# Sinkhorn attention and token mixer on one core: 21 idle TensorE products in place of 8 in the opening

## The chip, the cores and the metric

The kernel runs on one core of a Trainium2 chip. The metric is the device time of one execution in microseconds (us); of several runs the median counts. Inputs and output lie in the chip's DRAM as float32, and the kernel computes in bf16 with float32 accumulation.

## The reference, cut to what matters

```python
# q, k, v: (4, 8, 768, 64); sort_net: (4, 8, 8, 8); w_q, w_k: (512, 64); w_out: (512, 512)
P = sort_net
for _ in range(5):
    P = exp(P - max(P, -1)); P = P / sum(P, -1); P = P / sum(P, -2)
k_sorted = einsum('bhij,bhjcd->bhicd', P, k_blocks)      # 8 blocks of 96 rows
v_sorted = einsum('bhij,bhjcd->bhicd', P, v_blocks)
scores   = q_blocks @ k_sorted_blocks.T / 8
x        = softmax(scores) @ v_sorted_blocks             # heads side by side: (4, 768, 512)
wq, wk   = x @ w_q, x @ w_k
mixed    = (wq @ wk.T / 8) @ x
out      = relu(mixed) @ w_out
```

## The kernel before, in words

The work goes batch by batch (b = 0 to 3). For each batch the blocks of K and V of its eight heads are mixed by the sort matrix P, which is written as a 128-by-128 matrix M for each head, so that the mixing is one TensorE product per head and row group. The order of all work is written out by hand in the table `ORDER` (line 18). An entry names a step, the batch, a number, and, behind colons, an engine (A, D, G, S for ACT, DVE, POOL, SP) or a PSUM bank. A capital letter is a step of TensorE, a small letter mostly the step that follows it on another engine. Each engine runs its own entries strictly in the order of the table and waits for another engine only where data or a buffer is shared.

The prediction speaks only of the opening, batch 0, up to some 20 us. Its steps are:

- `c00` to `c05` (DVE) and `a01` to `a05` (ACT, the exponential): five rounds of normalising the 32 matrices of sort_net, one behind the other. The last, `c05`, ends with a transpose into `PbT` (line 208).
- `A00` (line 190): eight small products, which need `idb`, the identity that POOL makes.
- `Z0n:bank` (line 269): n products of `fil`, a zeroed piece of the tile `mixT`, 128x128 weights and 512 columns, into a PSUM bank. No step reads what they write. The number behind `Z0` is their count.
- `z10` to `z13` (POOL, and ACT for `z13`): casts of Q, head pair by head pair, into `Qn`; `Q00` to `Q03` (line 275): six transposes each on TensorE; `q00` to `q03`: their copies to `QT`.
- `U00`, `U01` (line 347): transposes of the weights w_q and w_k; `z01`, `z02` their copies on ACT.
- `B00` (line 247): eight small products of `PbT` and `Lx`, which spread P over 128 partitions, in bank 6; `n03, n00, n02, n01` (DVE, line 257): the four parts of `M`, from that bank.
- `Y03, Y00, Y02, Y01` (line 308): the sort matrix's products with V, 12 each, with casts `y03` and `y02` on ACT and `y00` and `y01` on DVE into a K-shaped tile `KT`; `u00` (ACT) keeps bank 6 as `PTR` for the later batches.
- `F00, F03` (line 314): eight transposes of that tile each, copied by `f00` (ACT) and `f03` (DVE) into `VT`.
- `K03, K00, K02, K01` (line 302): the sort matrix's products with K, 12 each, with casts `k03, k02` (ACT) and `k00, k01` (DVE). Then the scores `S`, the exponentials `e`, and so on through the batch.

All products are issued from one helper, `mm` (line 164), so all TensorE rows have L165; the copies have L169 (ACT), L171 (POOL) and L173 (DVE). K, V and Q of each batch, and the weights, are loaded by POOL's DMA queue (`u_l`, line 233), one load behind the other; SP's queue brings sort_net and Q of batch 0, sends the sorted V of the later batches from `Vs` into `VT`, and writes the output.

```python
    def u_Z(b, n, bank):
        w, x = (idb, wqk.rearrange("p t d -> p (t d)")) if b else (fil[:, 0:P], fil)
        for _ in range(n):
            mm(PS[:, bank, :], w, x)
```

Of the kernel before, what the change touches and what calls it, by code (L numbers as in the profile page):

```python
# [15 lines left out]
SPQ = 2  # L16

ORDER = """
i02:D i00:G c00:D a01:A i03:G A00:3 Z04:2 Z02:0 c01:D lp a02:A:3 c02:D a03:A lv0 lk0 c03:D z10:G
a04:A Q00:5 q00:A:5 Z02:6 c04:D U00:0 z13:A z11:G lv1 Q01:4 a05:A z01:A:0 q01:A:4 c05:D Q03:1 U01:3  # L20
z12:G q03:D:1 Q02:2 B00:6 z02:A:3 n03:D:6 n00:D:6 Y03:0 n02:D:6 Y00:4 q02:A:2 y03:A:0 n01:D:6
u00:A:6 y00:D:4 Y02:2 Y01:0 F00:4 y02:A:2 F03:5 K03:6 K00:2 y01:D:0 f03:D:5 K02:0 f00:A:4 k03:A:6
k02:A:0 k00:D:2 K01:4 S05:6 S06:2 e05:A:6 e06:A:2 k01:D:4 F02:0 S04:4 F01:1 lk1 S03:6 e04:A:4 P04:2
lq1 S02:4 e03:A:6 n11:D f02:D:0 lk2 lv2 e02:A:4 n10:G f01:D:1 r04:D:2 V12:0 V11:6 x04:D:2 v11:A:6
# [702 lines left out]
```

## Time and profile before

| | |
|---|---|
| time, median of 3 runs | 98.2 us (97.89 to 98.4) |
| the profiled execution's own time | 98.7 us |
| its span in the profile | 96.5 us |
| TensorE products (PE) | busy 86.2 us, 89% of the span |
| ACT | busy 72.9 us, 76% |
| DVE | busy 70.9 us, 73% |
| read from DRAM, written | 20.19 MB, 6.29 MB |

The span is the time from the first to the last instruction that the profiler saw; the rest of the execution's time lies around it. Times in the rows are counted from the start of the span. A row of the timeline gives start, length, engine, line, operation, what is written and read, shape and count; the bracket at its end is idle time of the engine just before, and what ended it. A matmul's recorded length includes the time for its result to come out, so a group of n products is n times their spacing, and a tail.

### The profile page before, as it was taken

The numbers are of one execution on the slowest core, as the hardware profiler recorded it, in microseconds if no ns is written. First come the engines' busy times: TensorE is split into PE (matmuls) and PEld (weight loads), VectorE is DVE, ScalarE is ACT, GpSimd is POOL, SyncE is SP. The second block draws the span as 40 slices with busy tenths as digits, with TensorE's granted clock in tenths as the row PEclk, the third lists the DMA queues.
The fourth block names the chain that finished last, engine by engine and source line by source line (L and its number), as shares of the span: only waits on it lengthen the run. The fifth ranks groups of instructions, "written<-read, shape, count | busy, mean of one in ns | idle before, by whom it ended". The sixth has DMA issues, their size and how long they took to land.

```text
span 96.5 us, 3360 instructions
## 1 busy us (share of the span) xinstructions
PE 86.2 (89%) x1416; PEld 61.0 (63%) x1416; DVE 70.9 (73%) x137; ACT 72.9 (76%) x106; POOL 25.8 (27%) x48
## 2 busy tenths in 40 slices
PE   4709979999999988999999999999999999999950
PEld 2105879787889677885855877786576465554430
DVE  2677777899998699898942799968899782657010
ACT  5236956999897997895999978998981787648640
POOL 7986997100018991000000000000200182000000
PEclk9999999999999999999999999999999999999999
DMA  0899999999999999999999999684783369383983
GB/s 7 272 385 201 203 204 203 206 203 208 202 221 249 250 208 205 206 208 211 238 253 225 203 205 123 150 283 132 200 312 143 91 196 404 127 329 138 385 323 140
DMA packets 22351, 20.88 MB, mean 216 GB/s; under 512 B 5056, under 2 KB 20416, under 8 KB 22336
## 3 DMA queue, kind: packets, MB, share of 16 engines
q0 software_dynamic: 12256, 9.31, 62.3%
q1 hardware_dynamic: 9792, 10.83, 34.8%
q10 hardware_dynamic: 288, 0.52, 1.5%
q8 instruction: 11, 0.18, 0.7%
q14 instruction: 4, 0.03, 0.1%
HBM read 20.19 MB, written 6.29 MB: 274 GB/s over the span
## 4 chain that ended last, share of the span: by engine, by line
PE 69%; DVE 19%; ACT 3%; issue 3%; DMA 2%; ACTq 0%; DVEq 0%
PE ps L165 69%; DVE X L409 4%; DMA ot<-in_sort_net_dram 2%; DVE Pm L201 1%; DVE tmp L204 1%; ACT Pm L183 1%; DVE Vs L173 1%; DVE qkT L173 1%; DVE tmp L199 1%; DVE tmp L200 1%; DVE tmp L205 1%; ACT E L380 1%; DVE KT L173 1%; ACT ot L169 1%; DVE QT L173 1%
## 5 line engine op out<-in xcount | busy, mean ns | idle before, releaser
L380 ACT ACTIVATE E<-ps 96x960 bf16<-96x960 f32 (+1 forms) x28 | 23.8, 903 | 1.7 <-PE ps L165 1.5
L165 PE MATMUL ps<-wo,mixT 128*128 128x512 bf16 (+1 forms) x100 | 23.3, 371 | 0.0
L409 DVE TENSOR_TENSOR X<-ps,Rall 96x896 bf16<-96x896 f32 (+1 forms) x20 | 19.8, 1002 | 0.5
L165 PEld LDWEIGHTS <-mixT 128*128 128x128 bf16 x108 | 9.8, 101 | 10.0 <-issue 1.5
L169 ACT COPY ot<-ps 128x512 f32<-128x512 f32 (+2 forms) x18 | 10.3, 575 | 5.1 <-PE ps L165 4.9
L169 ACT CAST KT<-ps 128x768 bf16<-128x768 f32 x13 | 10.1, 804 | 2.3 <-PE ps L165 2.2
L165 PE MATMUL ps<-idb,Qn 128*64 128x128 bf16 (+1 forms) x168 | 8.5, 234 | 3.1 <-POOL Qn L171 3.1
L173 DVE COPY ot<-ps 128x512 f32<-128x512 f32 (+1 forms) x8 | 5.3, 657 | 7.8 <-PE ps L165 6.5
L165 PEld LDWEIGHTS <-KT 64*128 64x128 bf16 (+1 forms) x288 | 8.7, 98 | 3.3 <-issue 1.9
L165 PE MATMUL ps<-VT,E 96*128 96x65 bf16 x256 | 10.6, 193 | 0.2 <-DMA VT<-Vs 0.2
L165 PEld LDWEIGHTS <-E 96*128 96x128 bf16 x256 | 9.2, 97 | 2.4 <-issue 0.7
L165 PE MATMUL ps<-QT,KT 64*128 64x96 bf16 x256 | 9.3, 204 | 0.6 <-DVE wk L173 0.3
L165 PEld LDWEIGHTS <-Qn 128*64 128x64 bf16 (+1 forms) x168 | 6.9, 114 | 4.6 <-POOL Qn L171 4.0
L472 ACT ACTIVATE mixT<-ps 128x1024 bf16<-128x1024 f32 x7 | 7.2, 1030 | 2.6 <-PE ps L165 2.6
L171 POOL COPY qD<-qkT 64x384 bf16<-64x384 bf16 x1 | 0.5, 499 | 31.6 <-ACT qkT L169 31.6
L265 POOL TENSOR_TENSOR M<-PTR,m_p 128x512 bf16<-128x512 bf16 x4 | 5.2, 1310 | 12.4 <-PE ps L165 11.8
L173 DVE CAST KT<-ps 128x768 bf16<-128x768 f32 x7 | 6.5, 954 | 1.2 <-PE ps L165 1.2
L165 PE MATMUL ps<-M,Kn 128*64 128x128 bf16 x192 | 6.9, 221 | 0.2 <-DVE X L409 0.2
L173 DVE COPY QT<-ps 128x768 bf16<-128x768 bf16 x10 | 5.3, 549 | 1.8 <-PE ps L165 1.8
L474 DVE TENSOR_SCALAR mixT<-ps 128x1024 bf16<-128x1024 f32 x5 | 6.1, 1223 | 0.6 <-PE ps L165 0.4
L165 PEld LDWEIGHTS <-Kn 128*64 128x64 bf16 x192 | 5.8, 110 | 1.0 <-issue 0.4
L169 ACT CAST Vs<-ps 128x1024 bf16<-128x1024 f32 x6 | 5.9, 1013 | 0.3 <-PE ps L165 0.3
(86 smaller groups left out, 133.7 us busy)
## 6 DMA issues: line engine op xcount, KB each, us to landing
out_dram<-ot SPq DMA_DIRECT2D x9, 512.0 KB, 3.4
Vn<-in_v_dram POOLq DMA_DIRECT2D x4, 768.0 KB, 17.9
Kn<-in_k_dram POOLq DMA_DIRECT2D x4, 768.0 KB, 17.4
VT<-Vs SPq DMA_DIRECT2D x18, 132.0 KB, 5.9
Qn<-in_q_dram POOLq DMA_DIRECT2D x3, 768.0 KB, 16.8
XT<-in_q_dram SPq DMA_DIRECT2D x2, 768.0 KB, 5.5
out_dram<-ot SPq DMA_DIRECT2D x4, 256.0 KB, 2.2
wo<-in_moe_w_out_dram POOLq DMA_DIRECT2D x1, 512.0 KB, 25.1
```

The costliest lines, as they stand in the source:

```text
L165: nc.tensor.matmul(o, w, x, is_transpose=t, start=start, stop=stop, skip_group_check=True)
L169: nc.scalar.copy(o, i)
L173: nc.vector.tensor_copy(o, i)
L183: nc.scalar.activation(Pv, Pq[n - 1], ACT.Exp)
L199: nc.vector.reduce_sum(tmp, Pv, axis=AX.X)
L200: nc.vector.reciprocal(tmp, tmp)
L201: nc.vector.tensor_mul(Pv, Pv, rows(tmp))
L265: ENG[e].tensor_tensor(out=M[b % 2][:, h0:h0 + hn], in0=src.unsqueeze(2).to_broadcast([P, hn, SP, NB]), in1=m_p.unsqueeze(1).unsqueeze(3). ...
L380: nc.scalar.activation(E[b % 2][:, n, 0:2 * w * BLK].rearrange("p (t a c) -> p a t c", a=2, c=BLK), PS[0:BLK, bank:bank + 2, 0:w * BLK].re ...
L409: nc.vector.tensor_mul(xo.rearrange("p (a t d) -> p a t d", a=2, d=D), avps(bank, w)[:, :, :, 0:D], Rall[:, b, n, :, 0:w].unsqueeze(3).to_ ...
L472: nc.scalar.activation(o, i, ACT.Relu)
L474: nc.vector.tensor_relu(o, i)
```

## The change

Only the table is edited. `Z04:2` becomes `Z09:2`, so that nine idle products stand there in place of four, and four entries `Z02:7` are new, each two idle products into bank 7: behind `Z02:0`, behind `Q03`, behind `Q02` (ahead of `B00`), and behind `B00` (ahead of `Y03`). With `Z02:0` and `Z02:6`, which stay, that makes 21 products in place of 8. Nothing else is added, removed or moved.

```diff
-i02:D i00:G c00:D a01:A i03:G A00:3 Z04:2 Z02:0 c01:D lp a02:A:3 c02:D a03:A lv0 lk0 c03:D z10:G
-a04:A Q00:5 q00:A:5 Z02:6 c04:D U00:0 z13:A z11:G lv1 Q01:4 a05:A z01:A:0 q01:A:4 c05:D Q03:1 U01:3
-z12:G q03:D:1 Q02:2 B00:6 z02:A:3 n03:D:6 n00:D:6 Y03:0 n02:D:6 Y00:4 q02:A:2 y03:A:0 n01:D:6
+i02:D i00:G c00:D a01:A i03:G A00:3 Z09:2 Z02:0 Z02:7 c01:D lp a02:A:3 c02:D a03:A lv0 lk0 c03:D z10:G
+a04:A Q00:5 q00:A:5 Z02:6 c04:D U00:0 z13:A z11:G lv1 Q01:4 a05:A z01:A:0 q01:A:4 c05:D Q03:1 Z02:7 U01:3
+z12:G q03:D:1 Q02:2 Z02:7 B00:6 Z02:7 z02:A:3 n03:D:6 n00:D:6 Y03:0 n02:D:6 Y00:4 q02:A:2 y03:A:0 n01:D:6
```

On TensorE (PE), between the transposes of Q's fourth head pair (`Q03`, rows that read `Qn_73`) and those of the weights (`U01`, rows that read `ot_71`), the instructions now stand so; the idle products are the rows that read `mixT_105`:

```order
 L165 LDWEIGHTS Qn_73
 L165 MATMUL ps<-idb,Qn_73 128x128
+L165 LDWEIGHTS mixT_105
+L165 MATMUL ps<-mixT_105 128x512
+L165 LDWEIGHTS mixT_105
+L165 MATMUL ps<-mixT_105 128x512
 L165 LDWEIGHTS ot_71
 L165 MATMUL ps<-idb,ot_71 128x128
```

One pair of idle products, each with its load of weights, now stands ahead of `U01` on PE; what follows keeps its order.

On PE again, ahead of `B00` (rows that read `PbT` and `Lx`) and behind `Q02`:

```order
 L165 LDWEIGHTS Qn_73
 L165 MATMUL ps<-idb,Qn_73 128x128
+L165 LDWEIGHTS mixT_105
+L165 MATMUL ps<-mixT_105 128x512
+L165 LDWEIGHTS mixT_105
+L165 MATMUL ps<-mixT_105 128x512
 L165 LDWEIGHTS Lx
 L165 MATMUL ps<-PbT,Lx 128x32
```

A second pair now stands between the last transpose of Q and the first product that needs `PbT`.

And on PE between the end of `B00` and the first product of `Y03` (rows that read `M_109` and `Vn_79`):

```order
 L165 LDWEIGHTS Lx
 L165 MATMUL ps<-PbT,Lx 128x32
+L165 LDWEIGHTS mixT_105
+L165 MATMUL ps<-mixT_105 128x512
+L165 LDWEIGHTS mixT_105
+L165 MATMUL ps<-mixT_105 128x512
 L165 LDWEIGHTS Vn_79
 L165 MATMUL ps<-M_109,Vn_79 64x128
```

A third pair now stands ahead of the sort matrix's products with V. The orders of DVE and ACT are the same as before.

## The prediction

> **What bounds the kernel now.** I read the chain of waits first, then TensorE's timeline of the opening. The chain, in order of time (start, length, what), from the end of the normalising rounds on:
>
> ```profile
> 11.89 0.23 DVE PbT L208
> ...
> 12.58 0.43 DVE M L265
> 13.06 4.84 PE ps L165 x88
> ...
> 41.80 13.97 PE ps L165 x284
> 55.78 36.25 PE ps L165 x468
> ```
>
> Until 12.1 us the chain is DVE and ACT normalising sort_net, with TensorE a bystander; from 13.06 us it is mostly TensorE, and from 41.80 us TensorE alone (13.97 + 36.25 us). So time won in the opening can last to the end only if it is won behind 13.06 us, and if no transfer eats it later. TensorE's timeline of the opening:
>
> ```profile
> 1.60 2.72 PE L165 MATMUL ps<-mixT 128*128 128x512 bf16 x6
> 7.38 0.82 PE L165 MATMUL ps<-idb,Qn 128*128 128x128 bf16 x6 [3.06 <-POOL Qn L171]
> 7.99 1.06 PE L165 MATMUL ps<-mixT 128*128 128x512 bf16 x2
> ...
> 9.55 1.46 PE L165 MATMUL ps<-idb,Qn 128*128 128x128 bf16 x12
> ...
> 11.23 0.85 PE L165 MATMUL ps<-idb,Qn 128*128 128x128 bf16 x6
> 12.17 0.37 PE L165 MATMUL ps<-PbT,Lx 32*128 32x32 bf16 x8
> 13.06 2.77 PE L165 MATMUL ps<-M,Vn 128*64 128x128 bf16 x48 [0.51 <-DVE M L265]
> 15.76 1.33 PE L165 MATMUL ps<-idb,KT 128*96 128x128 bf16 x16
> 17.01 1.53 PE L165 MATMUL ps<-M,Kn 128*64 128x128 bf16 x48
> ```
>
> The same 48 products of the same shape take 2.77 us with V at 13.06 and 1.53 us with K at 17.01. One by one (minimum, median, maximum in ns), here the V products and the K products, and then the transposes between them:
>
> ```profile
> L165 PE MATMUL ps<-M,Vn x48: 265/312/314, 13.1 to 15.5; 128*64 128x128 bf16 x48
> ...
> L165 PE MATMUL ps<-M,Kn x96: 216/219/243, 17.0 to 30.0; 128*64 128x128 bf16 x96
> ...
> L165 PE MATMUL ps<-idb,KT x16: 219/219/343, 15.8 to 16.9; 128*96 128x128 bf16 x16
> ```
>
> The array changes pace inside those 16 transposes, around 16.3 us: the first takes 343 ns and most take 219. Spacing is a group's length less one tail, over the count less one: (2.77 - 0.31)/47 = 0.052 us slow, (1.53 - 0.22)/47 = 0.028 us fast. For an idle product it is (2.72 - 0.63)/5 = 0.42 us slow, and for the same shape late in the kernel (2.75 - 0.38)/11 = 0.215 us:
>
> ```profile
> L165 PE MATMUL ps<-mixT x8: 587/634/634, 1.6 to 8.4; 128*128 128x512 bf16 x8
> ...
> 73.42 2.75 PE L165 MATMUL ps<-wo,mixT 128*128 128x512 bf16 x12
> L165 PE MATMUL ps<-wo,mixT x100: 272/379/390, 44.4 to 92.6; 128*128 128x512 bf16 x92, 128*128 128x256 bf16 x8
> ```
>
> So the array runs at half pace until it has been in dense use for about 3.2 us (13.06 to 16.3). The granted clock does not show it: the table by stretches has 1.00 for the idle products and for the V products alike (columns: sum, PE busy, granted clock, DMA share, GB/s).
>
> ```profile
> 1.60:4.32 2.72, 2.72 (x12) 1.00 0.59 174
> 13.06:15.83 2.77, 2.77 (x49) 1.00 1.32 204
> ```
>
> The Trainium skill, "TensorE: Matmul & The Clock Gate", Part 1, says that an array that has been idle passes half of its clock, that about 3.4 us of sustained use bring the full clock, and that the window is free-running. The rows agree in factor and length; the clock column does not show it.
>
> **The change, part by part.**
>
> *The first group.* Seven products more at 1.60 us make 13 in a row at the slow spacing: 12 x 0.42 + 0.63 = 5.7 us, to 7.3 us. They fill the 3.06 us in which PE waited for POOL's cast, and `Q00` starts at 7.38 us, so their cost is nothing; without that cover 7 x 0.42 = 2.9 us. Its own start hangs on the cast, as the bracket of its row shows. What they bring: 5.7 us of dense products, longer than the 3.2 us behind which the pace doubled. If use alone sets the pace, it changes at about 5 us, and the last of them are over by 6 to 6.5 us.
>
> *The second group (`Z02:6`, kept).* At the fast spacing two products are 0.43 us in place of 0.84, and `U00` then waits for its weights, of which the later part was issued at 3.61 and took 4.9 us, to 8.5. No gain: the copies behind it stand in ACT's queue behind `a04` and `z13`.
>
> *The pairs behind `Q03`, `Q02` and `B00`.* Fast, each is 0.43 us. `U01` waits for ACT's `z01` (10.20 + 0.56 = 10.76 us), and `Q03`, which can start when its cast is done at 9.9 us, ends its issue some 0.4 us later, so the pair (10.3 to 10.7) is covered. `Q02` (cast ended 11.02) goes from 11.05 to 11.4, its pair to 11.85; `B00` waits for `PbT` until 12.12 us: covered. `B00` takes until 12.4, its pair until 12.85; `Y03` waits for `M` until 13.02 us: covered. All three at nothing, if the pace is fast.
>
> ```profile
> 3.61 0.54 POOL L236 DMA_DIRECT2D ot<-in_moe_w_k_dram  x1
> DMA to landing us min/median/max: 4.9/5.2/5.5
> ...
> 9.04 0.83 ACT L169 CAST Qn<-XT 128x768 bf16<-128x768 f32 x1
> 10.20 0.82 POOL L171 CAST Qn<-XT 128x768 bf16<-128x768 f32 x1
> 10.20 0.56 ACT L169 COPY ot<-ps 128x512 bf16<-128x512 bf16 x1
> ...
> 12.58 1.42 DVE L265 TENSOR_TENSOR M<-ps,m_p 128x256 bf16<-128x256 f32 x4
> 14.66 0.96 DVE L173 CAST KT<-ps 128x768 bf16<-128x768 f32 x1 [0.66 <-PE ps L165]
> 15.94 0.96 DVE L173 CAST KT<-ps 128x768 bf16<-128x768 f32 x1 [0.32 <-PE ps L165]
> ```
>
> *What the fast pace is worth behind 13.06 us.* Nothing ahead of 13.06 moves, since DVE sets it. `Y03`, 12 products, ends at 13.06 + 11 x 0.052 + 0.31 = 13.94 us now, and at 13.06 + 11 x 0.028 + 0.22 = 13.59 fast. DVE's first cast waits 0.66 us for `Y00`; fast, that wait is gone, it starts when `M` is done (12.58 + 1.42 = 14.0 us) and ends at 14.96 in place of 15.62. The second follows at once, at 14.96 in place of 15.94. `F00` starts at 15.1 in place of 15.76. Its 16 transposes with `F03` go at the spacing that eight later ones show, (0.65 - 0.22)/7 = 0.061 us, and end their issue at 15.1 + 16 x 0.061 = 16.1 us, so `K03` would be 0.9 us early. But its K comes by DMA, issued at 5.04 and landing 11.2 us later, at 16.24 us:
>
> ```profile
> 19.19 0.65 PE L165 MATMUL ps<-idb,KT 128*96 128x128 bf16 x8
> ...
> 5.04 0.90 POOL L244 DMA_DIRECT2D Kn<-in_k_dram  x1
> DMA to landing us min/median/max: 11.2/11.2/11.2
> ```
>
> So `K03` starts at 16.3 in place of 17.01: 0.7 us. From there both kernels run at the fast pace, and the lead is carried or lost, not enlarged.
>
> *What could eat it.* V of batch 1 was issued at 9.13 and took 11.7 us, to 20.8; it is used at 21.75, at 21.05 with the lead. V of batch 2, issued at 13.58, took 25.4 us, to 38.98; it is used at 39.70, at 39.0 with the lead: just free. The sorted V of batch 1 goes through SP's queue and PE waits 0.17 us for it at 35.44; its sends start at 24.00 behind DVE's and ACT's copies, so they start earlier by the same lead. I carry the whole 0.7 us; bounds are 0 (a transfer eats all) and 0.98 (the lead of the second cast, if K landed sooner).
>
> ```profile
> 9.13 0.89 POOL L244 DMA_DIRECT2D Vn<-in_v_dram  x1
> DMA to landing us min/median/max: 11.7/11.7/11.7
> ...
> 13.58 0.90 POOL L244 DMA_DIRECT2D Vn<-in_v_dram  x1
> DMA to landing us min/median/max: 25.4/25.4/25.4
> ...
> 21.75 1.07 PE L165 MATMUL ps<-Vn,M 128*128 128x128 bf16 x16
> 35.44 0.85 PE L165 MATMUL ps<-VT,E 96*128 96x65 bf16 x22 [0.17 <-DMA VT<-Vs]
> 39.70 0.61 PE L165 MATMUL ps<-Vn,M 128*128 128x128 bf16 x8
> ```
>
> The sum: the profiled execution's 98.7 us (span 96.5) less 0.7 is 98.0 (span 95.8). Its time lies 0.5 us above the median of the runs shown, so for the median 98.2 - 0.7 = 97.5 us.
>
> **The rivals.**
>
> *Slower: the array is slow again, or still, where the pairs stand.* Between 7.4 and 12.4 us nearly all of TensorE's work is transposes, with idle stretches, and in the run of before 9.55 to 12.5 us of almost unbroken transposes did not bring the fast pace: the V products at 13.06 are slow. That speaks for it: transposes may not hold the pace either. Against it: from 16.3 us on, transposes among products never lost it, and the pairs put products among them. The Trainium skill, same page, Part 4, says that transposes do not count as use in the same way. By that rule the pace would fall back and this rival would hold. The price at the slow spacing: each pair is 2 x 0.42 = 0.84 us. `U01` and `Q02` come 0.84 late, `Q02`'s issue, which ends at 11.23 + 0.85 - 0.2 = 11.88 now, and its pair end at 11.88 + 2 x 0.84 = 13.56, where `B00` starts in place of 12.17, `M` 1.4 us late, and the pair behind `B00` puts `Y03` at 13.56 + 0.21 + 0.84 = 14.6, 1.55 us late. Some 0.25 us comes back, since more of V's products then fall behind the change of pace. That is 1.3 us: 99.5 us. It decides as soon as two products take more than the 0.45 us that the waits cover.
>
> *No change: the lead is eaten.* The array is fast at 13 us, but K of batch 0 lands later, or the sorted V of batch 1 lands at 35.4 us whatever SP does, since all sends share the DMA engines with POOL's loads. For it: the wait of 0.17 us stands there with no slack. Against it: all six sends hang on copies that come earlier. A form of this is that the runs shown, 0.5 us under the profiled one, had the fast pace earlier already. The lead that is left is then 0.1 us or less: 98.1 us.
>
> **How the numbers follow.** Forecast 0.62, slower rival 0.19, no change 0.19. About 0.5% (0.5 us) is what a measurement of this kernel can tell from no change. The forecast's own range is 97.0 (0.98 gained, and the 0.2 us by which the runs shown scatter) to 97.8. To hold 8 in 10 it must reach over the case of no change and the scatter of it, to 98.7, and leaves out most of the slower rival. Faster by over 0.5%: 0.60, all but a small part of the forecast. Within: 0.20. Slower: 0.20.
>
> **What would show it.** In the changed kernel's profile, the idle products of the first group should change from 634 ns to about 380 on the way, near 5 to 6 us; the transposes of Q should take about 219 ns in place of 314; the V products 219 in place of 312, as 48 in about 1.6 us or in pieces that wait for `M`; `Y03` should start within 0.05 us of 13.06, and `K03` near 16.3 us with its start released by the DMA of K. DVE's waits of 0.66 and 0.32 us should be gone. If the V products show 312 ns, or `B00` starts behind 12.3 us, the slower rival holds; if they show 219 and the wait at 35.44 us grows to 0.8, the second.

## The result, and the profile after

The change made the kernel slower: 99.14 us median (98.53 to 99.81, 15 runs) against 98.4 us (97.89 to 99.64, 15 runs) for the kernel before; the ratio is 1.0065, with a 95% interval of 1.0038 to 1.0092. The forecast was 97.5 us, and at most 98.7. The execution that was profiled after the change is the slowest of its 15, so the times lost in it are at the large end.

| | before | after |
|---|---|---|
| profiled execution's own time | 98.7 us | 99.81 us |
| its span | 96.5 us | 97.6 us |
| V products start | 13.06 us, slow | 13.20 us, fast |
| K products (`K03`) start | 17.01 us | 16.22 us |
| products of wq and wk behind the first scores of batch 1 start | 31.61 us | 32.36 us |

TensorE's timeline of the opening, after, and the idle products and V products one by one (minimum, median, maximum in ns):

```profile
1.60 5.08 PE L165 MATMUL ps<-mixT 128*128 128x512 bf16 x13
7.54 0.51 PE L165 MATMUL ps<-idb,Qn 128*128 128x128 bf16 x6 [0.85 <-POOL Qn L171]
12.34 0.35 PE L165 MATMUL ps<-PbT,Lx 32*128 32x32 bf16 x8 [0.16 <-DVE PbT L208]
13.20 1.20 PE L165 MATMUL ps<-M,Vn 128*64 128x128 bf16 x36
15.18 1.09 PE L165 MATMUL ps<-idb,KT 128*96 128x128 bf16 x16
16.22 1.53 PE L165 MATMUL ps<-M,Kn 128*64 128x128 bf16 x48
...
L165 PE MATMUL ps<-mixT x21: 379/427/634, 1.6 to 12.8; 128*128 128x512 bf16 x21
L165 PE MATMUL ps<-M,Vn x48: 216/219/243, 13.2 to 14.9; 128*64 128x128 bf16 x48
```

Up to here the forecast holds. The idle products pass from 634 to 379 ns within the first group, the V products take 219 ns in place of 312, and `K03` starts 17.01 - 16.22 = 0.79 us earlier. DVE's chain of normalising rounds ended 0.16 us later in this execution (sort_net landed later), and the lead was won all the same.

Then it goes. This is who TensorE waited for behind 13 us, before and after (us in total, times, longest):

```profile
PE ps L165 <- DVE X L409: 0.6, 3, 0.2
PE ps L165 <- DVE M L265: 0.5, 1, 0.5
PE ps L165 <- DVE wk L173: 0.3, 1, 0.3
PE ps L165 <- DVE Vs L173: 0.2, 1, 0.2
PE ps L165 <- DMA VT<-Vs: 0.2, 1, 0.2
```

```profile
PE ps L165 <- issue: 1.6, 3, 1.0
PE ps L165 <- DVE X L409: 0.7, 3, 0.3
PE ps L165 <- DVE wk L173: 0.3, 1, 0.3
PE ps L165 <- DVE Vs L173: 0.2, 1, 0.2
PE ps L165 <- ACT KT L169: 0.2, 1, 0.2
```

The first row of the second list is new: 1.6 us, in three pieces, in which TensorE waited for nothing that the profile shows. The chain of waits of the changed kernel, the work that ended last followed back from the end, has all three on it:

```profile
25.47 0.23 issue
25.70 0.71 PE ps L165 x14
...
31.19 0.98 issue
32.17 3.92 PE ps L165 x70
...
51.60 0.35 issue
```

The middle one stands between two steps of score products, `S15` (10) and `S16` (4), which run on in one piece of 14 in the profile before:

```profile
30.80 0.39 PE L165 MATMUL ps<-QT,KT 64*128 64x96 bf16 x10
32.17 0.26 PE L165 MATMUL ps<-QT,KT 64*128 64x96 bf16 x4 [0.98 <-issue]
```

```profile
31.20 0.47 PE L165 MATMUL ps<-QT,KT 64*128 64x96 bf16 x14
```

Between two steps a buffer might be missing, though no releaser is shown. The third stop leaves no room for that: it falls inside a step, behind the fourth of the ten products of `S20`, the last of three score steps, and all ten read the same piece of `KT` and of `QT` and write the same banks.

```profile
50.91 0.68 PE L165 MATMUL ps<-QT,KT 64*128 64x96 bf16 x24
51.94 0.30 PE L165 MATMUL ps<-QT,KT 64*128 64x96 bf16 x6 [0.35 <-issue]
```

What the stops have in common is their distance. From the end of the first to the end of the second TensorE issued 128 products and 128 loads of weights, 256 instructions, as the table by stretches counts them (busy time and count for PE, PEld, DVE, ACT, POOL; then granted clock, DMA share, GB/s):

```profile
25.70:32.16 6.46, 5.06 (x128) 4.40 (x128) 4.93 (x9) 5.56 (x8) 3.58 (x4) 1.00 1.24 238
```

From there to the third are 3 x 256, give or take one: 382 products and 383 loads in the same table, and the trace has four semaphore instructions there, which the table leaves out. In other kernels of this case the stop near 31 us stands behind the same count, whatever the step. Up to it TensorE has issued 479 products and 479 loads in the change, in the kernel with the first group alone, and in the one with 24 instructions fewer than before (both below). What it was about to issue was a score product in the first, a product of wq and wk in the second, a transpose of Q in the third:

```profile
0.00:31.30 31.30, 26.77 (x479) 19.01 (x479) 25.55 (x66) 22.87 (x35) 17.31 (x36) 1.00 1.16 214
0.00:31.55 31.55, 25.27 (x479) 18.84 (x479) 25.46 (x66) 23.33 (x36) 18.02 (x36) 1.00 1.16 214
0.00:33.20 33.20, 26.61 (x479) 20.11 (x479) 26.90 (x69) 24.87 (x37) 19.35 (x38) 1.00 1.16 215
```

The page's list of DMA queues has one of its own for instructions, and it moved 0.18 MB in 11 packets in both kernels, some 16 KB each:

```profile
q8 instruction: 11, 0.18, 0.7%
```

In a stretch from 29.8 to 30.3 us of the changed kernel one of them goes out, beside 142 packets of loads and stores:

```profile
q0 software_dynamic: 72, 0.06, 70.2%
q1 hardware_dynamic: 70, 0.06, 48.2%
q8 instruction: 1, 0.02, 11.0%
```

That packet takes 0.88 us (11.0% of 16 engines in 0.5 us), in the trace from 29.83 to 30.70 us. TensorE came to the end of its block of 256 instructions at 31.19 us and went on at 32.17 us, 1.47 us behind the packet's end. The other stops agree: in the kept traces all 15 of them end 1.3 to 1.7 us behind the end of their packet, and no border is crossed sooner behind its packet than that. The Trainium skill, "Runtime: NRT & Kernel Launch", section "Instruction fetch mechanics", says that an engine's instructions are refilled in blocks of 16 KiB, 256 instructions, the next while the current one runs, and that crossing a border is mostly hidden. The block size agrees with the distances here; the hiding holds in the kernel before, which has no such stop, and fails in the change, with 1.6 us at three borders.

From this came theory F: 26 instructions more, added early, put every later block border 13 products earlier in the program, and each border where TensorE is fast then costs what its block is late. The rivals were P, that the pairs of idle products cost the time, and T, that a data transfer eats any lead.

### The profile page after: what moved, and what is told of

It is laid out like the page before. It is cut to its first block, busy times and chain, and to the rows that moved or that the text cites. A ratio compares the mean times of both kernels' runs of the same rounds, so it can differ in the third digit from the quotient of the medians.

```text
span 97.6 us, 3386 instructions
## 1 busy us (share of the span) xinstructions
PE 87.4 (90%) x1429; PEld 59.4 (61%) x1429; DVE 70.7 (72%) x137; ACT 72.8 (75%) x106; POOL 25.8 (26%) x48
## 4 chain that ended last, share of the span: by engine, by line
PE 68%; DVE 17%; ACT 5%; issue 4%; DMA 2%; ACTq 0%; DVEq 0%
PE ps L165 68%; DVE X L409 3%; ACT E L380 2%; DVE KT L173 2%; DMA ot<-in_sort_net_dram 2%; DVE M L265 1%; DVE Pm L201 1%; DVE tmp L204 1%; ACT Pm L183 1%; DVE Vs L173 1%; DVE tmp L199 1%; DVE tmp L200 1%; DVE tmp L205 1%; ACT ot L169 1%; DVE ot L206 1%
## 5 line engine op out<-in xcount | busy, mean ns | idle before, releaser
L165 PEld LDWEIGHTS <-mixT 128*128 128x128 bf16 x121 | 11.1, 102 | 11.8 <-issue 3.2
L165 PE MATMUL ps<-idb,Qn 128*64 128x128 bf16 (+1 forms) x168 | 7.5, 221 | 1.6 <-POOL Qn L171 1.4
L165 PEld LDWEIGHTS <-Qn 128*64 128x64 bf16 (+1 forms) x168 | 5.8, 108 | 2.9 <-POOL Qn L171 2.1
L165 PE MATMUL ps<-mixT 128*128 128x512 bf16 x21 | 7.5, 501 | 0.0
L173 DVE CAST qkT<-ps 128x384 bf16<-128x384 f32 x5 | 2.8, 557 | 5.2 <-PE ps L165 5.1
```

What stands on the lines that cost most here:

```text
L165: nc.tensor.matmul(o, w, x, is_transpose=t, start=start, stop=stop, skip_group_check=True)
L173: nc.vector.tensor_copy(o, i)
```

## The experiments

**First group only.** The change without its three pairs.

```diff
-... Q03:1 Z02:7 U01:3
+... Q03:1 U01:3
-z12:G q03:D:1 Q02:2 Z02:7 B00:6 Z02:7 z02:A:3 ...
+z12:G q03:D:1 Q02:2 B00:6 z02:A:3 ...
```

> Only the first group of the change (13 idle products ahead of Q00, 15 in all), without the three pairs: 14 TensorE instructions more than before, not 26. Theory F (TensorE's instructions arrive in blocks of 256, each fetched by a transfer that stands in line with the loads; every instruction added early moves all later block borders to an earlier place in the program, and TensorE stands still at a border until the block is there): V products at about 219 ns, K03 near 16.2 us, a stall at the border near 31 us smaller than the 1.19 us of the change; 98.6 to 98.9 us. Rival P (the pairs themselves cost the time): the lead of 0.8 us reaches the end, 97.6 us. Rival T (a data transfer eats the lead whatever the count): 98.3 us.

Measured: 98.94 us, ratio 1.0046 (1.0016 to 1.0076). The pairs are not the cost: without them, P's gain does not come. TensorE waited 1.0 us for nothing shown, 0.7 at most at once. With 14 instructions more in place of 26, the stop near 31 us stands six products later in the program than in the change, inside the step of wq and wk.

**Count only.** The kernel before, with a step `X` of products as narrow as `A00`'s, in the places of the added idle products.

```diff
+    def u_X(b, n, bank):
+        for _ in range(n):
+            mm(PS[:, bank, 0:SP], fil[:, 0:P], fil[:, 0:SP])
-... Z04:2 Z02:0 c01:D ...   Q03:1 U01:3      Q02:2 B00:6 z02:A:3
+... Z04:2 Z02:0 X07:7 c01:D ...   Q03:1 X02:7 U01:3      Q02:2 X02:7 B00:6 X02:7 z02:A:3
```

> The kernel before with 13 products of 16 columns at the places where the change has its 13 added products: the same instruction count and order of kinds as the change, next to no array time (13 x 0.027 us). The pace should change at 16 us as before, with no lead at K03 (17.0 us). Theory F: borders lie where they lie in the change, so TensorE stalls at the border near 32 us by some 0.7 us; 98.9 to 99.3 us. Rivals P and T (pace, idle products or data transfers decide): 98.4 us, no change.

Measured: 99.32 us, ratio 1.0114 (1.0062 to 1.0165). Instructions with next to no array time cost what the change costs, and more. One part of the expectation fell: in the profiled execution the V products were fast (219 ns), so the pace does not always change at 16 us; `K03` started at 16.28 us, and the lead was lost at the borders nevertheless:

```profile
PE ps L165 <- issue: 1.1, 2, 0.5
...
31.41 0.26 PE L165 MATMUL ps<-QT,KT 64*128 64x96 bf16 x4 [0.55 <-issue]
```

It is the same place of the program as in the change, ahead of the four products of `S16`.

**Pace only.** The rival form of the gain: idle products in place of `A00`, and no instruction more than before.

```diff
-i02:D i00:G c00:D a01:A i03:G A00:3 Z04:2 Z02:0 c01:D ...
+i02:D i00:G i05:D c00:D a01:A i03:G Z014:2 c01:D ...
+        elif n == 5:
+            with nc.allow_low_precision(reason="sums of 0 and 1"):
+                nc.vector.reduce_sum(m_p, idb.rearrange("p (j s) -> p s j", s=SP), axis=AX.X)
-            nc.scalar.copy(m_p, PS[:, bank, 0:SP])
+            pass
```

> The pace without the count: A00 (eight small products that make m_p) is done by one DVE reduction instead, and the eight places go to idle products, 14 ahead of Q00 and 2 behind it; TensorE has exactly as many instructions as before. Theory F: K03 near 16.2 us as in the change, borders at the same place of the program as before, stalls of 0.3 us or less in all near 26 and 32 us; 97.7 to 98.0 us. Rival T: the lead is lost by 36 us all the same, 98.4 us. Rival P: 97.6 us, as there are no pairs.

Measured: 98.25 us, ratio 0.9994 (0.9964 to 1.0023): no change. Theory F and P missed; the time is near T's, but not for T's reason, since there was hardly a lead to lose (`K03` at 16.76 us, 0.25 early). The profile shows why. The transposes of Q ran fast and the V products behind them slow:

```profile
L165 PE MATMUL ps<-idb,Qn x24: 219/220/231, 7.3 to 11.3; 128*128 128x128 bf16 x24
...
L165 PE MATMUL ps<-M,Vn x48: 266/314/317, 13.0 to 15.5; 128*64 128x128 bf16 x48
```

The pace was won by 7.3 us and lost again ahead of the V products. The table by stretches shows it (granted clock in the third column from the end):

```profile
12.40:15.80 3.40, 2.89 (x53) 2.76 (x50) 2.50 (x6) 1.89 (x4) 2.79 (x4) 0.50 1.31 203
```

That is the slower rival's mechanism, in a kernel without pairs. One such stretch takes 0.5 x 3.4 / 96.2 from the mean granted clock of the execution, which is 0.982. Taken as a mark of a pace won and lost, a mean below 0.99 stands in 7 of 12 executions of this kernel, in 9 of 12 of the first-group kernel, in 4 of 23 of the kernel before in the same set, and in none of the 27 executions of the change in its two sets. So the pairs make such a loss rarer. They don't rule it out: the version that keeps the count, below, has them, and the mark in 2 of 10. Nor does the mark say that the V products were slow (see the count added late). The Trainium skill, "TensorE: Matmul & The Clock Gate", Part 4, says that transposes do not count as use in the same way. That the pace was lost among transposes agrees; but their 219 ns show that they do run at the fast pace when it is there, and in the profile of the count added late the pace came back at 11.4 us, behind 2.9 us of transposes and hardly a gap. Here idle stretches of 0.2 to 0.8 us stood among them. They are the likelier cause, though no experiment separates the two.

**Count tripled.** As the count-only kernel, with `X033:7` in place of `X07:7`.

> As the count-only kernel, but with 39 products of 16 columns in place of 13 (78 instructions more than before), 33 of them in the idle stretch ahead of Q00 (0.9 us of 3.06). Theory F: the borders lie 39 products earlier than before, and the time of a block under load (some 6 us for 256 instructions) makes 78/256 x 6 = 1.8 us, part of it covered; 99.6 to 100.4 us. Rivals P and T: 98.4 us, no change.

Measured: 99.63 us, ratio 1.0123 (1.0082 to 1.0164). The time is as theory F says, but the profile does not give it the credit: the waits for nothing shown are 0.3 us, and 1.2 us went at `K03`, whose load landed 12.2 us after its issue in place of 11.2. Why that load was late was not tried. Inconclusive on the cause.

**The pace held, the count kept.** The change with its instructions paid for: `A00` done as in the pace-only kernel, four products in `B00` for eight, and 12 idle products in the first group.

```diff
-... A00:3 Z09:2 Z02:0 Z02:7 c01:D ...
+... Z08:2 Z02:0 Z02:7 c01:D ...
-        for i in range(NB):
-            g, x = divmod(i, BH // NB)
-            mm(PS[:, bank, i * BH:(i + 1) * BH], Lx[:, x].rearrange("p j s -> p (j s)"),
-               PbT[:, g * BH:(g + 1) * BH])
+        X4 = BH // NB
+        o = PS[:, bank, 0:NB * BH].rearrange("p (g x h) -> p x g h", x=X4, h=BH)
+        for x in range(X4):
+            mm(o[:, x], Lx[:, x].rearrange("p j s -> p (j s)"), PbT)
```

> The change with its instructions paid for: A00 (8 products) is done by one DVE reduction, B00 is four products of 64 columns in place of eight of 32, and the first group has 12 products, not 13; the pairs stay. TensorE has exactly the 2834 rows of the kernel before, and the pace is fast and held to 13 us by the pairs. Theory F (block borders): K03 near 16.3 us, later borders at the same place of the program as before, so that most of the 0.7 us lead lasts: 97.6 to 97.9 us. Rival P (the pairs or the fast pace themselves cost the time later): 98.6 us or more. Rival T (transfers of data eat any lead): 98.3 us.

Measured: 97.93 us, ratio 0.9936 (0.9895 to 0.9977), faster than both kernels; the span of its profile is 95.8 us. This is the forecast of the prediction, a lead of 0.7 us that lasts, once the count is as before. Its list of TensorE's waits behind 13 us has no piece without a releaser, and the 14 score products stand in one piece again:

```profile
PE ps L165 <- DVE X L412: 0.4, 2, 0.2
PE ps L165 <- DMA VT<-Vs: 0.2, 1, 0.2
PE ps L165 <- DMA Kn<-in_k_dram: 0.2, 1, 0.2
...
30.52 0.47 PE L165 MATMUL ps<-QT,KT 64*128 64x96 bf16 x14
```

The wait for K at `K03` (16.34 us) is the one that the prediction put there.

Why the place of a border matters can be read off the same trace. The border that costs 0.98 us in the change stands here 26 instructions later in the program. The eight long products of wq and wk (1.47 us) then fall ahead of it, so the 256 instructions up to it take 6.25 us to run (26.09 to 32.34 us), as in the kernel before; in the change they take 5.49 us (25.70 to 31.19). The packets go out at nearly the same time, 29.97 us here and 29.83 in the change.

**Fewer instructions.** The kernel before with only the savings (`A00` and `B00` as above), 24 instructions fewer.

> Only the saving: A00 by DVE and B00 in four products, idle products as before (8); TensorE has 24 instructions fewer than before and no lead at K03 from the pace unless the window of the clock happens to fall well. Theory F: later borders lie 12 products later in the program; before stood still by 0.2 us or so at such borders, so 98.0 to 98.3 us. Rivals P and T: 98.3 us.

Measured: 98.58 us, ratio 0.9975 (0.993 to 1.002), above the expected 98.0 to 98.3 us, which decides nothing by itself. Its profile is the surprise: with fewer instructions it stands at borders too, where the profile before shows no stop (the expectation had put some 0.2 us there), and loses the lead that its fast V products (219 ns) gave.

```profile
PE ps L165 <- issue: 1.1, 3, 0.5
PE ps L165 <- DVE M L268: 0.5, 1, 0.5
PE ps L165 <- DMA VT<-Vs: 0.5, 1, 0.5
```

So theory F in the form "fewer is better" falls. What is left is that the place of the borders decides: moved 13 products earlier or 12 later, they fall where TensorE runs through a block faster than the next arrives.

**The count added late.** The same 13 narrow products (of `idb`) in the kernel before, ahead of `H31`, when the loads are over: `s20:S X013:7 H31:6`.

> The kernel before with 13 products of 16 columns added late, ahead of the products H31 near 77 us, when the loads are over: the same 26 instructions as in the count-only kernel, at a place where a block's transfer no longer stands in line. Theory F: no stall but their own array time (13 x 0.027 = 0.35 us at most); 98.3 to 98.7 us. Rival (26 more instructions cost about 1 us wherever they stand): 99.3 us.

Measured: 98.61 us, ratio 1.0006 (0.9962 to 1.0051). Late, 26 instructions cost nothing that can be seen; early they cost 1.1%. The kernel is the same as before up to 77 us, and this execution had its V products fast:

```profile
L165 PE MATMUL ps<-M,Vn x48: 217/219/244, 13.0 to 14.7; 128*64 128x128 bf16 x48
```

`K03` started at 16.05 us, 0.96 earlier than in the profile before. So the kernel before has the lead in some of its executions, without the change. The mean granted clock of this execution is 0.982, yet its V products were fast: the pace was lost from 8.0 to 11.4 us and was back ahead of them.

**The border moved back.** The version that keeps the count, with `X013:7` behind its first group.

> The version that keeps the count (12 idle products in the first group, pairs, A00 and B00 shortened) with 13 products of 16 columns more in the idle stretch ahead of Q00: nothing but 26 instructions, so that the block borders lie where they lie in the change. Theory F: the stalls of the change come back (1 us near 31 us, 0.3 us near 51 us), 98.6 to 99.2 us. Rival (the shorter A00 and B00 were what helped): 97.9 us, as without them.

Measured: 98.59 us, ratio 1.002 (0.9989 to 1.0052), against 0.9936 without the 13 narrow products: 26 instructions take back 0.8%, and the stop is where it was in the change. The time is at the lower edge of the expected 98.6 to 99.2 us, and the stops are shorter than in the change, 0.7 us in all.

```profile
PE ps L165 <- issue: 0.7, 2, 0.6
...
30.52 0.39 PE L165 MATMUL ps<-QT,KT 64*128 64x96 bf16 x10
31.47 0.26 PE L165 MATMUL ps<-QT,KT 64*128 64x96 bf16 x4 [0.56 <-issue]
```

The two ratios come from different sets, each against the kernel before on its own chip. In the set of this kernel the next one, which has the count of the kernel before (and its pairs emptied), has 0.9956, and the intervals do not meet.

**The pairs emptied.** The version that keeps the count, with two narrow products for each pair: `Q03:1 X02:7 U01:3`, `Q02:2 X02:7 B00:6 X02:7`.

> The version that keeps the count, with each of the three pairs replaced by two products of 16 columns: same instructions, same borders, but no array time in the pairs. If the pairs hold the fast pace, it is lost in some executions before the V products (as in the pace-only kernel's profile), and the median lies between that version and before: 98.0 to 98.4 us. If the first group alone brings it and it lasts: 97.9 us.

Measured: 98.07 us, ratio 0.9956 (0.9925 to 0.9987). The interval overlaps that of the version with pairs; 4 of 12 executions have a mean granted clock under 0.99, against 2 of 10. In the one that was profiled (98.6 us) the V products took 314 ns, and `K03` started at 17.04 us, with no lead. What the pairs add to the first group is small and not settled.

**One whole block more.** The kernel before with `X0128:7` behind its first group.

> The kernel before with 128 products of 16 columns in the idle stretch ahead of Q00 (3.5 us of array time, some 0.5 us more than the stretch, covered by waits of ACT and DVE): 256 instructions more, one whole block, so that every later border lies at the same place of the program as before. Theory F in the form 'the place of the borders decides': 98.3 to 98.7 us. In the form 'every instruction costs its share of a block' or with any cost per instruction as the count-only kernels show (1.0 us for 26): well over 100 us.

Measured: 98.87 us, ratio 1.0049 (1.001 to 1.0088). That is 0.2 us above the expectation of 98.3 to 98.7 us; where it goes was not followed up. The one profile kept is of an execution of 100.46 us, at half pace from 12.2 to 19.0 us; TensorE has no stop without a releaser in it, but it can't stand for the others. Yet 256 instructions in the opening cost half of what 26 cost there (0.5% against 1.1%), and no price per instruction gives that; borders at the same places of the program do.

**The change again.**

> The change itself once more, on the chip of this set, for a comparison with the version that keeps its count: 98.9 to 99.2 us, with stalls of 0.3 us and more at borders 256 instructions apart.

Measured: 99.2 us, ratio 1.0068 (1.0037 to 1.0099), with two waits for nothing shown, 1.1 us together.

## Why the prediction was wrong

*The first group, and the pace.* Right: the pace changed inside the first group, and `Q00` was not held up (7.54 us, released by POOL's cast). The rule behind it, about 3.2 us of dense use, is not borne out: the count-late kernel, the same as before up to 77 us, ran `Q00` fast (219 ns) behind 2.7 us of idle products.

*The pairs.* Right in what they take of the array, 0.43 us each in waits that were there. By the mean clock no execution of the change lost the pace, while 9 of 12 without the pairs did; that they always hold it is not shown (2 of 10 of the version that keeps the count).

*The lead at `K03`.* Right in place and size: 0.7 us forecast, 0.79 in the profile. That K's load bounds it shows in the version that keeps the count, where `K03` waits 0.2 us for it; in the change's profile no such wait is listed.

*"From there both kernels run at the fast pace, and the lead is carried or lost, not enlarged", and the list of what could eat it.* This is the step that failed, with the words "All three at nothing" ahead of it. The products were priced by their time in the array alone, and the eaters looked for were transfers of data. The supply of instructions was not among them: 26 instructions more put the block borders elsewhere, and in the profiled execution TensorE stood there for 1.6 us, which is the lead twice over (1.1 us when the change was run again). The count-only kernel (1.0114 with no array time to speak of), the version that keeps the count (0.9936) and the same version with its border moved back (1.002) show it.

*"For the median 98.2 - 0.7".* Partly wrong as well: the lead was reckoned against a profiled execution with slow V products, at 98.7 us, while the kernel before has them fast in some of its executions, as the count-late kernel's profile shows. The prediction named that as a form of "no change" and gave it little. How often it happens can't be told from the runs: only profiled executions show when the products were fast.

*The rivals.* The slower rival gave the right sign by a mechanism that did not act in the change; the pace-only kernel shows it acting where there are no pairs. The no-change rival looked in the right stretch, ahead of 36 us, at the wrong transfers.

What stays open: why the block that was wanted at 31 us came no earlier. The traces show its packet going out among loads and stores, 2.4 to 4.7 us after TensorE had crossed the border before, at all borders ahead of 53 us; behind 57 us, where POOL's loads run out, it is 2.3 us at most. And the same instructions cost nothing when added after the loads. That the line of loads delays the packet is argued from that, and not shown by a kernel with fewer loads. What fills the 1.3 to 1.7 us from the packet's end to TensorE's next instruction is not shown either.

## What to carry to other kernels

An instruction has a place in a block as well as a duration: before adding or removing some early in a long unrolled program, find the block borders in the trace (stops "for nothing", 256 instructions apart) and see which products stand there after the edit, and how long the 256 instructions ahead of the border take: here 5.5 us were too few, and 6.25 us enough. Compare edits of TensorE's program at an equal count, or a good change may be hidden behind a border, as this one was (0.9936 with the count kept, in place of 1.0065). Idle products do bring the fast pace early, and a gain from it is to be measured over several executions, since the kernel without them sometimes has it too.

## What was not expected of the hardware

- The supply of instructions can bound TensorE: 256 instructions took 25.70 to 32.16 us, of which 0.98 us were a stop, while two other queues were sending; and TensorE goes on no sooner than 1.3 us behind the end of a block's packet.
- Transposes run at the fast pace (219 ns), and it can be lost among them and their idle stretches: 3.4 us at half pace in the pace-only kernel, right behind them.
